# Left-over rows of a mixture of experts in units of 32 instead of 128, in plain fp32, with four column groups of TensorE

## The chip, the cores and the metric

The kernel runs on one core of a Trainium2 chip. The metric is the device time of one execution in microseconds. A core has TensorE (matmuls; PE in the profile, and PEld for its weight loads), VectorE (DVE), ScalarE (ACT), GpSimd (POOL) and SyncE (SP, which here only issues transfers). Transfers between the chip's memory and the core go through queues to 16 DMA engines. A matmul holds one operand stationary (here up to 128 rows by 128 columns), streams the other, moving one past it (here up to 512 columns), and adds into one of the eight PSUM banks that the kernel uses.

## The reference

Two layers follow each other: a retention (a linear attention with decay) and a mixture of experts with one expert per token.

```python
# retention: q, k, v are (4, 8, 768, 64)
for t in range(S):
    state = gamma * state + einsum('bhd,bhe->bhde', k[:, :, t], v[:, :, t])
    y[:, :, t] = scale * einsum('bhd,bhde->bhe', q[:, :, t], state)
x = y.transpose(0, 2, 1, 3).reshape(3072, 512)

# mixture: 8 experts, w1 (8, 512, 1024), w2 (8, 1024, 512)
logits = x @ w_gate + modality_bias[modality_id]
e_idx = argmax(logits)
gate_w = softmax(logits)[e_idx]
for e in range(E):
    mask = e_idx == e
    h = maximum(x[mask] @ w1[e], 0)
    out[mask] = gate_w[mask] * (h @ w2[e])
```

All data are fp32. Which expert a token goes to is only known on the chip.

## The kernel before, in words

**Retention and routing.** The 3072 tokens are 24 chunks of 128. For each chunk the kernel computes scores (`sc`, line 188), the state (`st`, 249), the outputs (`y`, 209 and 215), and from them the tokens' rows and router logits (`x`, 232). These matmuls are plain fp32; those of lines 188, 209, 215 and 249 use halves or quarters of the array side by side. After every three chunks the rows are routed, and scattered into `x_dram`, a region in the chip's memory where each expert has its own run of rows. Each row carries its token's number and its gate weight behind the 512 values. Rows that fill up a piece are padded with zeros and a token number that is out of bounds (`pad_c`).

**Slots and units.** A candidate is a piece of 256 rows of one expert (12 per expert, 96 in all). At five points during the retention (`EVENTS`) the two best full pieces become jobs "e"; after the last chunk the two largest pieces that are left become slots "s0" and "s1" of 256 rows, and whatever is left then is listed in units "u" of 128 rows. The lists are computed on the chip (`final_a`, `final_m`, `final_b`): one-hot matrices by rank, summed by small matmuls into a row of integers. SP reads expert and position of each job from such a list into registers (`reg`, `start_job`).

**A job.** Matmuls of the experts run in fp32r, which is made accurate by splitting each operand into a high and a low part and adding three products (`PAIRS`). So each expert's weights are loaded as eight raw pieces of 512 KB (`raw`, line 576, four of w1 and four of w2; the transfer is skipped when the job before has the same expert), and each piece is cut (`cut`): a cast on ACT (`hi`, 580) and a subtraction on DVE (`lo`, 582). A slot's first layer (`first_slot`, 636) gives eight blocks of the hidden layer, transposed as they come, 12 matmuls each; its second layer (`second`, 682) does two halves of 128 rows, 24 matmuls each; the half is scaled by the gate weight on ACT (694) and scattered to the output by POOL (695). That makes 16 steps, counted as `t` from 0: 0 to 7 the first layer, 8 to 15 the second.

A unit job (`first_unit`) has its 128 rows stationary and the weights moving: four blocks of 12 matmuls (652), each followed by a relu on ACT (659), transposes on TensorE (`flip`, 671) and splits on ACT and DVE (594, 595), then the second layer over one half.

**What sets the order.** `tc.manual_schedule` keeps PE, ACT, DVE and SP in program order; each engine works its instructions off in that order and waits where it must. The program order is that of `run_job`: while job k goes through its steps, the next job's w1 is loaded at step 2 (after the register loads), its rows and its w2 at step 8, its rows are transposed at step 12 (`flip_x`, 621), its w1 is cut at steps 9, 11, 13, 15, and job k's own w2 at steps 0, 2, 4, 6. In a unit job the same things lie closer: loads at steps 0 and 4, the transposes at step 7, the cuts at steps 0 to 7. `raw` tiles exist once, so a load waits on SP until the piece before it has been cut, and all later loads wait behind it. In between, `tick` deals out the routing and list steps, and `next(ret)` the rest of the retention.

**The jobs:** ten "e", then s0, u0, s1, u1. The first `NTAIL = 2` units are such jobs; further ones would be done by a loop at the end of the program, `For_i(NTAIL, nun)`, whose number of turns is a value read from the list. PSUM has eight banks handed out in turn.

Of the kernel before, what the change touches and what calls it, by code (L numbers as in the profile page):

```python
# [7 lines left out]
F32 = mybir.dt.float32  # L8
# [7 lines left out]
P = 128  # L16
# [14 lines left out]
NEV = 2  # L31
NFIN = NSLOT - NEV * len(EVENTS)
NTAIL = 2
NUNIT = 40
DENSE = 10
# [11 lines left out]
def kernel(  # L47
# [351 lines left out]
    ex_c = cnd[:, 2:3]  # L399
    U = NUNIT  # L400

    def small(nm, shape, dt=F32):
# [5 lines left out]
    lc = {}  # L408
    lists = {}

    def list_consts():
# [6 lines left out]
        vals = small("vals", [NCAND, 3], BF16)  # L418
# [4 lines left out]
        nc.vector.tensor_copy(vals[:, 2:3], ex_c)  # L423
        onef = small("onef", [NCAND, NCAND])
# [10 lines left out]
        nc.gpsimd.memset(base_f[:, n : n + U], float(EMPTY))  # L435
        lc.update(ord_r=ord_r, vals=vals, onef=onef, base_e=base_e, base_f=base_f)
        mid["keep"] = keep
# [27 lines left out]
    def ranked():  # L465
# [5 lines left out]
        rank = passing("rank", [NCAND, 1])  # L471
        nc.vector.tensor_reduce(rank, gt, axis=AX.X, op=ALU.add)
        return size, rank

# [25 lines left out]
    def final_a():  # L500
        size, rank = ranked()
        ord_r = lc["ord_r"]
        h0 = small("h0", [NCAND, 1])
        nc.vector.tensor_scalar(h0, size, 0.0, None, op0=ALU.is_gt)
        h0b = small("h0b", [NCAND, 1], BF16)
        nc.vector.tensor_copy(h0b, h0)
# [4 lines left out]
        rku = small("rku", [NCAND, 1])  # L511
        nc.vector.tensor_scalar(rku, rank, float(NFIN), None, op0=ALU.subtract)
        h1 = small("h1", [NCAND, 1])
        nc.vector.tensor_scalar(h1, size, float(P), None, op0=ALU.is_gt)
        lft = small("lft", [NCAND, 1])
        nc.vector.tensor_scalar(lft, rku, 0.0, None, op0=ALU.is_ge)
        nc.vector.tensor_tensor(h1, h1, lft, op=ALU.mult)
        nc.vector.tensor_tensor(h0, h0, lft, op=ALU.mult)
        mid["f"] = (ohs, h0, h0b, h1, rku)

    def final_m():
        ohs, h0, h0b, h1, rku = mid.pop("f")
# [7 lines left out]
        rk1 = small("rk1", [NCAND, 1])  # L530
        nc.vector.scalar_tensor_tensor(
            rk1, pn[:NCAND, 0:1], float(-NFIN), rku, op0=ALU.add, op1=ALU.add
        )
        oh1 = small("oh1", [NCAND, U], BF16)
        nc.vector.tensor_scalar(oh1, ord_r, rk1, h1, op0=ALU.is_equal, op1=ALU.mult)
        h0c = small("h0c", [NCAND, 1], BF16)
        nc.vector.tensor_copy(h0c, h0)
        h1c = small("h1c", [NCAND, 1], BF16)
        nc.vector.tensor_copy(h1c, h1)
        mid["f"] = (ohs, oh0, oh1, h0c, h1c)  # L540

    def final_b():
        ohs, oh0, oh1, h0c, h1c = mid.pop("f")
        vals = lc["vals"]
# [7 lines left out]
        for i in range(3):  # L552
            mm(i * NFIN, NFIN, vals[:, i : i + 1], ohs, True, True)
        mm(n, U, vals[:, 0:1], oh0, True, False)
        mm(n, U, vals[:, 1:2], oh1, False, True)
        mm(n + U, U, vals[:, 2:3], oh0, True, False)
        mm(n + U, U, vals[:, 2:3], oh1, False, True)
        mm(n + 2 * U, 1, h0c, one, True, False)
        mm(n + 2 * U, 1, h1c, one, False, True)
        w = n + 2 * U + 1  # L560
# [82 lines left out]

    def first_unit(s):
        tag, hT = s["tag"], s.setdefault("hT", [])
        hs = []
        for i in range(4):
            ph = bank(f"uh{i}_{tag}")[:, :256]
            n = 0
            for kc in range(KC):  # L650
                for a, wi in PAIRS:
                    nc.tensor.matmul(
                        ph, s["xT"][kc // 2][a][:, kc % 2, :],
                        s["w1"][i][wi][:, kc * 256 : (kc + 1) * 256],
                        start=(n == 0), stop=(n == 3 * KC - 1),
                    )
                    n += 1
            t = me.tile([P, 256], F32, tag="hs", name=f"hs{i}_{tag}", bufs=2)
            nc.scalar.activation(t, ph, AF.Relu)
            hs.append(t)  # L660
            if i > 0:
                flip(tag, i - 1, hs[i - 1], hT)
            if i < 3:
                yield
        flip(tag, 3, hs[3], hT)
        yield

    def flip(tag, i, hs, hT):
        pb = bank(f"ut{i}_{tag}")
        for m in range(2):  # L670
            nc.tensor.transpose(pb[:, m * P : (m + 1) * P], hs[:, m * P : (m + 1) * P], ident)
        for m in range(2):
            hT.append(split("hT", 2 * i + m, pb[:, m * P : (m + 1) * P], [P, P]))

    def second(s):
        tag, hT = s["tag"], s["hT"]
        for hh in range(s["nh"]):
# [26 lines left out]
            )  # L704
            if tag != "dyn":
                disjoint(ins, "out_rows")
            yield

    def reg(lst, i, hi):
        return nc.values_load(lst[0:1, i : i + 1], engines=[SP], min_val=0, max_val=hi)  # L710

    def start_job(j):
        kind, g, i = j
        s = dict(tag=f"{kind}{g}{i}", nh=1 if kind == "u" else 2)
        if kind == "e":
            lst, at, n = lists[g], 0, NEV
            s["group"] = g
        elif kind == "s":
            lst, at, n = lists["final"], 0, NFIN
        else:  # L720
            lst, at, n = lists["final"], 3 * NFIN, U
        s["e"] = reg(lst, at + s["nh"] * n + i, NE - 1)
# [12 lines left out]
    def both(s):  # L735
        yield from first_slot(s) if s["nh"] == 2 else first_unit(s)
        yield from second(s)
# [3 lines left out]
    def run_job(k):  # L741
        cur = state_of[k]
        long = cur["nh"] == 2
        last = k + 1 == len(jobs)
        if not long:
            cuts = {t: (cur, 2, t) for t in range(4)}
        elif k == 0:
            cuts = {0: (cur, 1, 2), 1: (cur, 1, 3)}
# [4 lines left out]
        for t, _ in enumerate(both(cur)):  # L753
            if t == (2 if long else 0) and not last:
                nxt = state_of[k + 1] = start_job(jobs[k + 1])
                raw(nxt, 1, cur)
                for i in range(4):
                    cuts[9 + 2 * i if long else 4 + i] = (nxt, 1, i)
            if t in cuts:
                cut(*cuts[t])  # L760
            if not last:
                if t == (8 if long else 4):
                    rows_in(nxt)
                    raw(nxt, 2, cur)
                if t == (12 if long else 7):
                    flip_x(nxt)
# [102 lines left out]
    def everything():  # L869
# [11 lines left out]
        decay_v(0)  # L881
        ret = retention(modi)

        ahead = None
# [19 lines left out]
        for k in range(len(jobs)):  # L904
            for t, _ in enumerate(run_job(k)):
                if t % 2:
                    tick()
                if t % 3 == 1:
                    next(ret, None)
        assert next(ret, None) is None and not todo  # L910

# [6 lines left out]
    with tc.For_i(NTAIL, nun, 1) as iv:  # L918
# [3 lines left out]
        cd = nc.values_load(  # L922
            lst[0:1, bass.ds(iv + at, 1)], engines=[SP], min_val=0, max_val=EMPTY
        )
        s = dict(tag="dyn", nh=1, e=e, at=[cd])
        rows_in(s)
        raw(s, 1)
        raw(s, 2)
        flip_x(s)
        for m in (1, 2):  # L930
            for i in range(4):
                cut(s, m, i)
        for _ in both(s):
            pass
# [89 lines left out]
```

## Time and profile before

| | us |
|---|---|
| three runs: median, lowest, highest | 475.86, 470.4, 477.1 |
| the profiled execution: its own time | 472.48 |
| its span, first to last instruction | 470.5 |
| TensorE busy | 433.6 (92%) |
| VectorE busy | 287.0 (61%) |
| ScalarE busy | 205.9 (44%) |
| mean rate of the DMA engines | 182 GB/s |

The profile shows one execution. Its lines give start and duration in us, engine, source line, operation, `output<-inputs`, and in square brackets how long the engine stood idle before and for whom. `PEclk` is the TensorE clock that was granted, as a share of full speed. In tables by stretch the columns are: length of the stretch, then busy time and number of instructions for PE, PEld, DVE, ACT and POOL, the granted clock, the busy share of the DMA engines and GB/s. Matmuls are pipelined, so a record's duration (0.28 us) is longer than the spacing of two records (0.12 us); it is the spacing that tells what a matmul costs in a row of them. Records of tiles of job u0 and u1 carry the names `xp_u`, `uh_u`, `ut_u`, `o_u`; those of s0 and s1 end in `_s`, those of early jobs in `_e`.

### The profile page before, as it was taken

The numbers are of one execution on the slowest core, as the hardware profiler recorded it, in microseconds if no ns is written. First come the engines' busy times: TensorE is split into PE (matmuls) and PEld (weight loads), VectorE is DVE, ScalarE is ACT, GpSimd is POOL, SyncE is SP. The second block draws the span as 40 slices with busy tenths as digits, with TensorE's granted clock in tenths as the row PEclk, the third lists the DMA queues.
The fourth block names the chain that finished last, engine by engine and source line by source line (L and its number), as shares of the span: only waits on it lengthen the run. The fifth ranks groups of instructions, "written<-read, shape, count | busy, mean of one in ns | idle before, by whom it ended". The sixth has DMA issues, their size and how long they took to land.

```text
span 470.5 us, 10222 instructions
## 1 busy us (share of the span) xinstructions
PE 433.6 (92%) x3676; PEld 382.9 (81%) x3676; DVE 287.0 (61%) x648; ACT 205.9 (44%) x363; POOL 103.1 (22%) x130
## 2 busy tenths in 40 slices
PE   3997989998999999999999999979999999889980
PEld 3876879888889889879879889878989898779860
DVE  1787488658556856855765677436656564667350
ACT  1221135445335336245345455435646464755540
POOL 2225215023011310421141042760000000000100
PEclk9998689999999999999999999999999999989987
DMA  8993797933535683348412171724757313864100
GB/s 287 400 362 118 273 396 241 388 129 116 162 113 176 230 340 114 128 150 292 139 69 97 45 230 65 257 71 158 256 196 255 106 48 119 286 240 163 71 1 2
DMA packets 27860, 85.70 MB, mean 182 GB/s; under 512 B 5278, under 2 KB 5406, under 8 KB 27808
## 3 DMA queue, kind: packets, MB, share of 16 engines
q1 hardware_dynamic: 22240, 70.50, 43.1%
q0 software_dynamic: 5280, 14.10, 7.9%
q8 instruction: 30, 0.49, 0.4%
q10 hardware_dynamic: 288, 0.43, 0.3%
q14 instruction: 22, 0.18, 0.1%
HBM read 91.61 MB, written 18.24 MB: 233 GB/s over the span
## 4 chain that ended last, share of the span: by engine, by line
PE 47%; issue 34%; DVE 6%; POOL 6%; DMA 3%; ACT 1%; POOLq 0%; ACTq 0%; DVEq 0%
PE h_e L636 13%; PE o_e L682 12%; PE sc L188 5%; PE x L232 5%; PE y L215 5%; POOL out_dram L695 3%; PE y L209 3%; POOL x_dram L386 3%; PE st L249 2%; DVE lo_e L582 2%; DMA kq<-in_qkv_dram 1%; DMA x_dram<-zer,pad_i 1%; PE xp_e L621 1%; ACT hi_e L580 1%; DVE a L193 1%
## 5 line engine op out<-in xcount | busy, mean ns | idle before, releaser
L582 DVE TENSOR_TENSOR lo_e<-raw,hi_e 128x1024 fp32r<-128x1024 f32 x80 | 98.1, 1226 | 66.7 <-ACT hi_e L580 57.1
L636 PE MATMUL h_e<-xTh,lo_e 128*128 128x256 f32 x320 | 91.4, 286 | 3.2 <-DVE lo_e L582 1.7
L636 PE MATMUL h_e<-xTh,hi_e 128*128 128x256 f32 x320 | 93.0, 290 | 0.5 <-issue 0.3
L636 PE MATMUL h_e<-xTl,hi_e 128*128 128x256 f32 x320 | 91.2, 285 | 0.7 <-issue 0.7
L580 ACT CAST hi_e<-raw 128x1024 fp32r<-128x1024 f32 x80 | 83.5, 1043 | 0.0
L682 PE MATMUL o_e<-hi_e,hTh 128*128 128x512 f32 x160 | 65.7, 411 | 0.0
L636 PEld LDWEIGHTS h_e<-xTh,lo_e 128*128 128x128 f32 x320 | 62.0, 194 | 3.4 <-DVE lo_e L582 2.3
L636 PEld LDWEIGHTS h_e<-xTh,hi_e 128*128 128x128 f32 x320 | 61.9, 193 | 2.9 <-issue 1.6
L636 PEld LDWEIGHTS h_e<-xTl,hi_e 128*128 128x128 f32 x320 | 61.9, 194 | 1.4 <-issue 1.3
L682 PE MATMUL o_e<-lo_e,hTh 128*128 128x512 f32 x160 | 62.7, 392 | 0.0
L682 PE MATMUL o_e<-hi_e,hTl 128*128 128x512 f32 x160 | 62.6, 391 | 0.0
L589 ACT ACTIVATE hTh<-h_e 128x256 fp32r<-128x256 f32 x80 | 30.6, 384 | 61.9 <-PE h_e L636 52.7
L779 POOL TENSOR_TENSOR vd<-kv,cst 128x512 f32<-128x512 f32 x24 | 25.4, 1060 | 107.8 <-PE y L215 59.1
L193 DVE TENSOR_TENSOR a<-sc,cst 128x512 f32<-128x512 f32 x48 | 30.8, 683 | 24.1 <-PE sc L188 24.0
L590 DVE SCALAR_TENSOR_TENSOR hTl<-h_e,hTh 128x256 fp32r<-128x256 f32 x80 | 33.3, 418 | 18.5 <-ACT hTh L589 18.1
L695 POOL DMA_INDIRECT out_dram<-o_e,xg_e x20 | 19.9, 995 | 111.1 <-ACT o_e L694 103.0
L694 ACT ACTIVATE o_e<-o_e,xg_e 128x512 f32<-128x512 f32 x20 | 13.8, 689 | 68.4 <-issue 36.7
L188 PE MATMUL sc<-kq 64*128 64x128 f32 x384 | 30.6, 303 | 7.5 <-DMA kq<-in_qkv_dram 7.5
L326 POOL DMA_INDIRECT x_dram<-xs,pos x24 | 29.3, 1220 | 33.1 <-DVE key L458 18.1
L682 PEld LDWEIGHTS o_e<-hi_e,hTh 128*128 128x128 f32 x160 | 30.1, 188 | 7.5 <-issue 1.4
L682 PEld LDWEIGHTS o_e<-lo_e,hTh 128*128 128x128 f32 x160 | 30.0, 188 | 6.7
L682 PEld LDWEIGHTS o_e<-hi_e,hTl 128*128 128x128 f32 x160 | 30.1, 188 | 5.2
(171 smaller groups left out, 724.4 us busy)
## 6 DMA issues: line engine op xcount, KB each, us to landing
raw<-in_w_dram SPq DMA_DIRECT2D x112, 512.0 KB
kv<-in_qkv_dram SPq DMA_DIRECT2D x24, 512.0 KB
kq<-in_qkv_dram SPq DMA_DIRECT2D x23, 512.0 KB
xg_e<-x_dram SPq DMA_DIRECT2D x20, 272.0 KB
xg_s<-x_dram SPq DMA_DIRECT2D x4, 272.0 KB
xg_u<-x_dram SPq DMA_DIRECT2D x2, 272.0 KB
x_dram<-xs,pos POOLq DMA_INDIRECT x24
out_dram<-o_e,xg_e POOLq DMA_INDIRECT x20
```

The costliest lines, as they stand in the source:

```text
L188: nc.tensor.matmul(pe[j][:, g * P : (g + 1) * P], kt[r, g], qt[r, g], start=True, stop=True, skip_group_check=True,)
L193: nc.vector.tensor_tensor(a[:, j], pe[j].rearrange("p (h t) -> p h t", t=P), mask.unsqueeze(1).to_broadcast([P, NG, P]), op=ALU.mult,)
L215: nc.tensor.matmul(py[j][g % 2 * D : (g % 2 + 1) * D, g // 2], vd[:, 2 * g + j], a[:, j, g], start=(s is None and g < 2), stop=(g >= 2), s ...
L326: ins = nc.gpsimd.indirect_dma_start(out=x_dram[:, :], out_offset=bass.IndirectOffsetOnAxis(ap=pos[:, i : i + 1], axis=0), in_=xs.rearrang ...
L580: nc.scalar.copy(hi, raws[m][i])
L582: nc.vector.tensor_tensor(lo, raws[m][i], hi.bitcast(F32), op=ALU.subtract)
L589: nc.scalar.activation(hi, src, AF.Relu)
L590: nc.vector.scalar_tensor_tensor(lo, src, 0.0, hi.bitcast(F32), op0=ALU.max, op1=ALU.subtract)
L636: nc.tensor.matmul(ph, s["w1"][f // 2][wi][:, o : o + P], s["xT"][kc // 2][a][:, kc % 2, :], start=(n == 0), stop=(n == 3 * KC - 1),)
L682: nc.tensor.matmul(po, hT[f][a][:, hh * P : (hh + 1) * P], s["w2"][f // 2][wi][:, (f % 2) * DM : (f % 2 + 1) * DM], start=(n == 0), stop=( ...
L695: ins = nc.gpsimd.indirect_dma_start(out=out[:, :], out_offset=bass.IndirectOffsetOnAxis(ap=xg.bitcast(I32)[:, 0, P : P + 1], axis=0), in_ ...
L779: ins = nc.gpsimd.tensor_tensor(vds[n], vv, dec[:, n % NCH].unsqueeze(2).to_broadcast([P, H, D]), op=ALU.mult)
```

## The change

Left-over rows are listed in units of 32 rows instead of 128, up to 144 of them, and a unit is no job any more. `jobs` holds the ten "e" and s0, s1; `first_unit`, `flip` and the unit's branches in `start_job` and `run_job` are removed. A new generator `unit` does one unit: it loads the expert's weights whole and unsplit into rooms that the retention used (`kq`, `kv`, `a`), and computes in plain fp32. The first layer's four quarters of 256 hidden columns go to four column groups of 32 (output partitions 0 to 31, 32 to 63, and so on of one bank), so that the hidden layer of 32 rows fills 128 partitions; the second layer's four partial sums come out in the same way, and a matmul with a constant 0/1 matrix `sel` adds the four groups. The main loop deals the unit's stages out: unit 0's loads at step 9 of the last early job, its stages at steps 3, 6, 8, 10, 12 of s0; unit 1's loads at step 9 of s0, its stages in s1. The loop at the end, for further units, calls the same generator without a slot beside it.

```diff
+UNIT = 32
 NTAIL = 2
-NUNIT = 40
+NUNIT = 144
...
+        nc.vector.tensor_reduce(
+            sel, ident.rearrange("p (j t) -> p t j", t=UNIT), axis=AX.X, op=ALU.add
+        )
...
     def final_m():
...
         pn = bank("pn")
-        one = ones[:NCAND, :NCAND]
-        nc.tensor.matmul(pn[:NCAND, 0:1], one, h0b, start=True, stop=True)
-        oh0 = small("oh0", [NCAND, U], BF16)
-        nc.vector.tensor_scalar(oh0, ord_r, rku, h0, op0=ALU.is_equal, op1=ALU.mult)
...
+        nc.tensor.matmul(pn[:NCAND, 0:1], mid.pop("lt"), numb, start=True, stop=True)
+        end = small("end", [NCAND, 1])
+        nc.vector.tensor_tensor(end, pn[:NCAND, 0:1], num, op=ALU.add)
+        first = small("first", [NCAND, 1])
+        nc.vector.tensor_copy(first, pn[:NCAND, 0:1])
...
+        ohu = small("ohu", [NCAND, U], BF16)
+        nc.vector.tensor_scalar(ohu, ord_r, first, None, op0=ALU.is_ge)
         nc.vector.scalar_tensor_tensor(
...
+            ohu, ord_r, end, ohu, op0=ALU.is_lt, op1=ALU.mult
+        )
+        at = small("at", [NCAND, U], BF16)
+        nc.vector.tensor_tensor(at, ohu, ord_r, op=ALU.mult)
...
+    def unit(tag, e, at):
+        wa = [ld.tile([P, QW], F32, tag="kq", name=f"wa{i}_{tag}", bufs=4) for i in range(4)]
+        wb = [ld.tile([P, QW], F32, tag="kv", name=f"wb{i}_{tag}", bufs=3) for i in range(3)]
+        wb.append(wk.tile([P, QW], F32, tag="a", name=f"wb3_{tag}"))
+        xu = wk.tile([UNIT, NG, P + NE], F32, tag="xs", name=f"xu_{tag}", bufs=6)
+        nc.sync.dma_start(
+            xu.rearrange("p g e -> p (g e)"), x_dram[bass.ds(at * UNIT, UNIT), :]
+        )
+        for src, w in ((w1, wa), (w2, wb)):
+            for i in range(4):
+                nc.sync.dma_start(w[i], src[bass.ds(e, 1), i].rearrange("o p f -> p (o f)"))
+        yield
+        pb = bank(f"ux_{tag}")[:, : KC * UNIT].rearrange("p (k t) -> p k t", k=KC)
+        for kc in range(KC):
+            nc.tensor.transpose(pb[:, kc], xu[:, kc, :P], ident[:UNIT, :UNIT])
+        xT = wk.tile([P, KC, UNIT], F32, tag="s", name=f"uxT_{tag}")
+        nc.vector.tensor_copy(xT, pb)
+        yield
+        ph = bank(f"uh_{tag}")
+        for kc in range(KC):
+            for j in range(4):
+                nc.tensor.matmul(
+                    ph[j * UNIT : (j + 1) * UNIT, :256], xT[:, kc],
+                    wa[j][:, kc * 256 : (kc + 1) * 256],
+                    start=(kc == 0), stop=(kc == KC - 1), skip_group_check=True,
+                )
+        hs = wk.tile([P, 256], F32, tag="s", name=f"uhs_{tag}")
+        nc.scalar.activation(hs, ph[:, :256], AF.Relu)
+        yield
+        pt = bank(f"ut_{tag}")
+        for m in range(2):
+            nc.tensor.transpose(pt[:, m * P : (m + 1) * P], hs[:, m * P : (m + 1) * P], ident)
+        hT = wk.tile([P, 2, P], F32, tag="s", name=f"uhT_{tag}")
+        nc.vector.tensor_copy(hT, pt[:, :256].rearrange("p (m t) -> p m t", m=2))
+        yield
+        po = bank(f"uo_{tag}")
+        for m in range(2):
+            for j in range(4):
+                nc.tensor.matmul(
+                    po[j * UNIT : (j + 1) * UNIT], hT[:, m, j * UNIT : (j + 1) * UNIT],
+                    wb[j][:, m * DM : (m + 1) * DM],
+                    start=(m == 0), stop=(m == 1), skip_group_check=True,
+                )
+        os = wk.tile([P, DM], F32, tag="yT", name=f"uos_{tag}")
+        nc.scalar.copy(os, po)
+        yield
+        pf = bank(f"uf_{tag}")[:UNIT]
+        nc.tensor.matmul(pf, sel, os, start=True, stop=True)
+        of = wk.tile([UNIT, DM], F32, tag="yT", name=f"uof_{tag}")
+        nc.scalar.activation(of, pf, AF.Copy, scale=xu[:, 0, P + 1 : P + 2])
+        ins = nc.gpsimd.indirect_dma_start(
...
     jobs = [("e", g, i) for g in EVENTS for i in range(NEV)]
-    for i in range(max(NFIN, NTAIL)):
-        jobs += [("s", 0, i)] * (i < NFIN) + [("u", 0, i)] * (i < NTAIL)
+    jobs += [("s", 0, i) for i in range(NFIN)]
+
+    steps = {}
+    for u in range(NTAIL):
+        k = len(jobs) - NTAIL + u
+        steps[k - 1, 9] = u
+        steps.update({(k, t): u for t in (3, 6, 8, 10, 12, 14)})
...
                 if t % 3 == 1:
                     next(ret, None)
+                if (k, t) in steps:
+                    u = steps[k, t]
+                    if u not in units:
+                        at = 3 * NFIN + u
+                        lst = lists["final"]
+                        units[u] = unit(
+                            f"u{u}", reg(lst, at + U, NE - 1), reg(lst, at, NCAND * UPS)
+                        )
+                    next(units[u], None)
...
     with tc.For_i(NTAIL, nun, 1) as iv:
...
-        for _ in both(s):
+        for _ in unit("dyn", e, cd):
             pass
```

The list steps `final_a`, `final_m` and `final_b` change with it: a piece of `size` rows gives as many units as there are multiples of 32 below `size`, and the units are numbered through by a matmul with the comparison matrix of the ranks.

More of the change, by code (lines that the diff above doesn't have):

```diff
@@ L533, in final_m @@
         )
[L534 to L540, printed above, removed]
+        at = small("at", [NCAND, U], BF16)
+        nc.vector.tensor_tensor(at, ohu, ord_r, op=ALU.mult)
+        mid["f"] = (ohs, numb, back, ohu, at)
@@ L542, in final_b @@
     def final_b():
-        ohs, oh0, oh1, h0c, h1c = mid.pop("f")
+        ohs, numb, back, ohu, at = mid.pop("f")
         vals = lc["vals"]
@@ L553, in final_b @@
             mm(i * NFIN, NFIN, vals[:, i : i + 1], ohs, True, True)
[L554 to L559, printed above, removed]
+        mm(n, U, vals[:, 3:4], ohu, True, False)
+        mm(n, U, one, at, False, False)
+        mm(n, U, back, ohu, False, True)
+        mm(n + U, U, vals[:, 2:3], ohu, True, True)
+        mm(n + 2 * U, 1, numb, one, True, True)
         w = n + 2 * U + 1
@@ L642, in first_slot @@
             yield
[L644 to L673, printed above, removed]
     def second(s):
@@ L713, in start_job @@
         kind, g, i = j
-        s = dict(tag=f"{kind}{g}{i}", nh=1 if kind == "u" else 2)
+        s = dict(tag=f"{kind}{g}{i}", nh=2)
         if kind == "e":
@@ L717, in start_job @@
             s["group"] = g
-        elif kind == "s":
+        else:
             lst, at, n = lists["final"], 0, NFIN
-        else:
-            lst, at, n = lists["final"], 3 * NFIN, U
         s["e"] = reg(lst, at + s["nh"] * n + i, NE - 1)
@@ L735, in both @@
     def both(s):
-        yield from first_slot(s) if s["nh"] == 2 else first_unit(s)
+        yield from first_slot(s)
         yield from second(s)
@@ L742, in run_job @@
         cur = state_of[k]
-        long = cur["nh"] == 2
         last = k + 1 == len(jobs)
-        if not long:
-            cuts = {t: (cur, 2, t) for t in range(4)}
-        elif k == 0:
+        if k == 0:
             cuts = {0: (cur, 1, 2), 1: (cur, 1, 3)}
@@ L753, in run_job @@
         for t, _ in enumerate(both(cur)):
-            if t == (2 if long else 0) and not last:
+            if t == 2 and not last:
                 nxt = state_of[k + 1] = start_job(jobs[k + 1])
@@ L757, in run_job @@
                 for i in range(4):
-                    cuts[9 + 2 * i if long else 4 + i] = (nxt, 1, i)
+                    cuts[9 + 2 * i] = (nxt, 1, i)
             if t in cuts:
@@ L882, in everything @@
         ret = retention(modi)
+        units = {}
         ahead = None
@@ L922 @@
         cd = nc.values_load(
-            lst[0:1, bass.ds(iv + at, 1)], engines=[SP], min_val=0, max_val=EMPTY
+            lst[0:1, bass.ds(iv + at, 1)], engines=[SP], min_val=0, max_val=NCAND * UPS
         )
[L925 to L932, printed above, removed]
-        for _ in both(s):
+        for _ in unit("dyn", e, cd):
             pass
```

55 lines of the change are left out of this document (36 added, 19 removed).

## The prediction, on record before the changed kernel was run

> **What bounds the kernel now.** I read the page first, then stretches of the end cut at the starts of its jobs, then TensorE's records in order, then the DMA issues.
>
> ```profile
> span 470.5 us, 10222 instructions
> PE 433.6 (92%) x3676; PEld 382.9 (81%) x3676; DVE 287.0 (61%) x648; ACT 205.9 (44%) x363; POOL 103.1 (22%) x130
> ...
> PEclk9998689999999999999999999999999999989987
> ```
>
> TensorE is busy 92% of the span and nobody else is near; its granted clock has dents only at the start and in the last slices. These hold the left-over jobs, so I cut there: job e9 (the last early slot), slot s0, unit u0, slot s1, unit u1, and what follows the last matmul.
>
> ```profile
> core 0: us, PE busy (x) PEld busy (x) DVE busy (x) ACT busy (x) POOL busy (x), PEclk, DMA share, GB/s
> 353.10:376.41 23.31, 23.31 (x153) 21.35 (x152) 13.67 (x18) 12.90 (x20) 1.96 (x2) 1.00 0.53 182
> 376.41:399.32 22.91, 22.91 (x149) 20.92 (x148) 13.13 (x18) 12.40 (x20) 1.96 (x2) 1.00 0.25 82
> 399.32:415.56 16.24, 13.97 (x82) 12.24 (x81) 11.04 (x16) 11.16 (x21) 0.98 (x1) 0.89 0.73 246
> 415.56:443.55 27.99, 25.80 (x157) 23.37 (x156) 15.06 (x21) 13.53 (x22) 1.96 (x2) 0.94 0.49 172
> 443.55:459.70 16.15, 13.91 (x81) 12.08 (x79) 8.08 (x13) 8.34 (x18) 0.98 (x1) 0.89 0.04 13
> 459.70:470.50 10.80, 0.16 (x1) 0.00 (x0) 0.00 (x0) 0.69 (x1) 0.98 (x1) 0.70 0.01 2
> ```
>
> A slot is 23.31 us of unbroken matmuls at full clock (e9). A unit holds TensorE for 16.2 us, and the slot after one takes 27.99. Where the extra goes is in TensorE's waits, and in what follows each of them:
>
> ```profile
> 408.17 0.44 PE L671 MATMUL ut_u<-cst,hs_u 128*128 128x128 f32 x2 [2.27 <-ACT hs_u L659]
> 417.92 0.38 PE L636 MATMUL h_s<-xTh,hi_s 128*128 128x256 f32 x1 [1.32 <-ACT xTh L594]
> 419.29 0.39 PE L636 MATMUL h_s<-xTl,hi_s 128*128 128x256 f32 x1 [0.87 <-DVE xTl L595]
> 452.34 0.44 PE L671 MATMUL ut_u<-cst,hs_u 128*128 128x128 f32 x2 [2.24 <-ACT hs_u L659]
> ```
>
> ```profile
> 409.46:412.87 3.41, 3.41 (x10) 2.67 (x9) 2.27 (x5) 3.02 (x6) 0.00 (x0) 0.51 0.51 169
> 419.70:423.11 3.41, 3.41 (x18) 3.41 (x18) 0.70 (x3) 1.32 (x2) 0.00 (x0) 0.51 0.87 319
> 453.83:457.24 3.41, 3.41 (x10) 2.67 (x9) 1.97 (x4) 1.31 (x3) 0.00 (x0) 0.51 0.00 0
> ```
>
> Each gap of about 2.2 us is followed by 3.41 us at a clock of 0.51, in which half, 1.7 us, is lost. So three gaps and three such stretches, some 6.7 + 5.1 us, stand in the end beside the units' own matmuls. TensorE's order bounds this end; what takes time out of its row between 376.41 and 459.70 comes off the span.
>
> **What falls away.** From 376.41 to the last matmul's end stand 22.91 + 16.24 + 27.99 + 16.15 = 83.29 us. Both 128-row units go, with 16 casts and 16 subtractions of their weights. Slot s1 now follows s0 directly, its rows transposed at s0's step 12 with steps 13 to 15 as cover, as in e9; the x wait at 417.92 goes with it. Two slots remain: s0 as e9, 23.31; s1 without a next job's 8 transposes:
>
> ```profile
> 348.09 1.04 PE L621 MATMUL xp_e<-cst,xg_e 128*128 128x128 f32 x8
> 348.89 0.48 PE L682 MATMUL o_e<-hi_e,hTh 128*128 128x512 f32 x1
> ```
>
> These take 348.89 - 348.09 = 0.80, so s1 is 22.51.
>
> **What comes: a unit of 32 on TensorE.** The trace has plain fp32 matmuls in the retention, full width and side by side:
>
> ```profile
> 115.29 0.93 PE x L232 x8
> 116.22 0.60 PE y L209 x16
> 116.81 1.02 PE y L215 x16
> 117.84 4.50 PE h_e L636 x36
> ```
>
> An fp32 matmul leaves two records (4 matmuls of line 232 are 8 records). Those of 128x128 by 136 columns go one after another: 0.93 / 8 / 136 = 0.855 ns per column and record. Line 215 has two groups of 64 columns over all 128 rows: 16 records of 128 columns would be 1.75 us alone and took 1.02, which is 8 rounds of pairs (0.875) and 0.15 on entering. Line 209 has four 64x64 quarters: 4 rounds (0.44) and 0.16. The 36 matmuls behind them took 4.50 where 36 spacings of 0.12 make 4.32, so coming back costs 0.18:
>
> ```profile
> 375.96 0.39 PE L682 MATMUL o_e<-hi_e,hTl 128*128 128x512 f32 x1
> 376.19 0.39 PE L682 MATMUL o_e<-lo_e,hTh 128*128 128x512 f32 x1
> ...
> 376.52 0.28 PE L636 MATMUL h_s<-xTh,lo_s 128*128 128x256 f32 x1
> 376.64 0.28 PE L636 MATMUL h_s<-xTl,hi_s 128*128 128x256 f32 x1
> ...
> 394.76 0.60 PE L621 MATMUL xp_u<-cst,xg_u 128*128 128x128 f32 x4
> 395.12 0.48 PE L682 MATMUL o_s<-hi_s,hTh 128*128 128x512 f32 x1
> ...
> 446.43 0.38 PE L671 MATMUL ut_u<-cst,hs_u 128*128 128x128 f32 x2
> 446.56 0.36 PE L652 MATMUL uh_u<-hi_u,xTh 128*128 128x256 f32 x1
> ```
>
> The unit, stage by stage, each with 0.16 to enter and 0.18 to return:
> - rows transposed: four, of 32 rows, at most the 0.36 of four full ones: 0.70
> - first layer: 16 matmuls are 32 records of 256 columns; four abreast, 8 rounds x 256 x 0.855 ns = 1.75: 2.09
> - hidden transposed: two, 0.13, and 0.1 after: 0.25
> - second layer: 8 matmuls are 16 records of 512 columns; four abreast, 4 rounds = 1.75: 2.09
> - the sum over the groups: 2 records of 512 columns = 0.88: 1.22
>
> Together U = 6.35 us. No row shows four groups of 32 over the same 128 rows. Bounds: everything abreast and free to enter, 4.9; pairs only, as line 215 shows, 3.5 us for each layer, U = 9.85; one after another 7.0 each, U = 16.85. I take four abreast: line 209 shows four in flight, and line 215 that groups sharing all rows do not hinder each other.
>
> On this the Trainium skill ("TensorE: Matmul & The Clock Gate", Part 3, Measured speedup vs the span model) has three column groups of 512 columns at 2.38x, not 3x. At that efficiency four would be 3.17x, each layer 2.2 us, and the sum would come out 1.8 us higher; an estimate from that page, and line 215's pairs (1.75 in 0.875 beside the entry) do better than it.
>
> **Copies on ACT and DVE.**
>
> ```profile
> L694 ACT ACTIVATE o_e<-o_e,xg_e 128x512 f32<-128x512 f32 x20 | 13.8, 689 | 68.4 <-issue 36.7
> ...
> L659 ACT ACTIVATE hs_u<-uh_u 128x256 f32<-128x256 f32 x8 | 3.1, 386 | 0.0
> L595 DVE TENSOR_TENSOR hTl<-ut_u,hTh 128x128 fp32r<-128x128 f32 x16 | 4.4, 287 | 2.7 <-ACT hTh L594 2.7
> ```
>
> A unit adds 0.39 + 2 x 0.69 on ACT and two copies on DVE of 0.29 to 0.42. ACT is busy 12.40 and DVE 13.13 of s0's 22.91, and between a unit's stages stand two steps of the slot (one of 12 spacings, 1.44, and six of 0.23, 1.4). The relu needs the cut and split ahead of it plus itself, some 1.9 us, and has 2.8. I cost these at nothing, covered by the slot's matmuls. Without that cover each of four copies per unit would hold TensorE about 1 us, 8 in all, and gaps that long would bring the half clock back.
>
> **The weights on SP's queue.**
>
> ```profile
> q1 hardware_dynamic: 22240, 70.50, 43.1%
> ...
> raw<-in_w_dram SPq DMA_DIRECT2D x112, 512.0 KB
> ...
> xg_u<-x_dram SPq DMA_DIRECT2D x2, 272.0 KB
> ```
>
> ```profile
> 10.00:20.00 10.00, 10.00 (x151) 8.98 (x148) 6.35 (x19) 1.89 (x5) 3.51 (x10) 1.00 1.04 397
> 20.00:30.00 10.00, 9.15 (x150) 7.96 (x151) 9.33 (x36) 2.40 (x7) 2.96 (x7) 1.00 1.03 408
> ```
>
> A unit adds its rows (70 KB) and eight loads of 512 KB, unconditional, behind slot s0's (or s1's) second-layer weights and ahead of the next slot's first-layer ones. The order is kept, so those next ones queue behind 4.2 MB: 10.5 us at 400 GB/s. u0's loads can start once s0's last w2 piece has its room, after e9's step 6 (about 364), and their rooms are free since the retention; they land near 376, wanted from s0's step 6 (near 387). Slot s1's w1 follows by about 382, wanted from step 9 (near 391); its w2 by 390, wanted from 406. u1's first rooms come free at u0's first layer (388), its second at u0's second layer (395); all land by 406 and are wanted from 416. Nothing sits behind u1's waits on SP. The early jobs see none of this. I cost the loads at nothing; if DMA gave 182 GB/s, the page's mean, the 13.2 MB from 365 on would land at 438 where the last are wanted near 425: 13 us.
>
> **Lists.** The final lists grow to 144 places and need some more DVE operations of this kind, once, near 280; TensorE's wait there now:
>
> ```profile
> 280.78 0.23 PE L550 MATMUL ptf<-oh,vals 96*1 96x40 bf16 x3 [0.22 <-DVE h0c L537]
> ```
>
> I add 0.4 for that and the new constant's reduction at the start, between 0 and 1.
>
> **The sum.** 472.48 (the profiled execution) - 83.29 + 23.31 + 22.51 + 2 x 6.35 + 0.4 = 448.1; I say 448. What follows the last matmul (10.80) and the 1.98 us outside the span stay, since the last output is again a 128-row one. The profiled execution is 3.4 below the median of the runs (475.86) and 2.1 above the fastest, so no correction.
>
> **How many units there are** decides whether the loop at the end runs. It does not now (no row of it; 112 loads are 14 jobs). Two units of 128 can be up to eight of 32. From the reference's own inputs I worked out the router's counts: 1567, 1502 and 3 rows. Six slots go to each large expert, the last of 222 rows; 31 and 3 rows are left: two units either way. The trace bears this out: 70.50 MB less 24 + 23.5 retention loads of 0.524 MB, 26 row loads of 0.279 and 0.6 of the rest leaves 37.7 MB = 72 pieces, nine loads of an expert, as many as this order of jobs has.
>
> **Rivals.**
> - *The groups do not run side by side.* Pairs: 448.1 + 2 x 3.5 = 455.1. One at a time: 448.1 + 2 x 10.5 = 469.1, no change that can be told. For it: no row with four over the same rows. Against: lines 215 and 209. The Trainium skill speaks for it ("TensorE: Matmul & The Clock Gate", Part 3, The mechanism): a weight load overlaps running matmuls only where the row group differs, and all groups here share their rows. The trace differs for pairs, 1.02 us against 1.75.
> - *Weights late*, as costed: 13 us, 461. Against: 397 and 408 GB/s in the profile.
> - *Slower: the loop runs.* Each further unit there is bare: 4.2 MB (10.5 us), U, copies of 2.4, and no cover, 21 us or more. One turn gives 469, two 490; from two on it is slower than before. For it: a unit is a quarter as large and there are still two in the schedule. Against: the counts.
>
> **How the numbers follow.** Forecast 0.72, pairs 0.10, one at a time 0.06, late weights 0.05, the loop twice or more 0.04, and 0.03 for something better than the forecast (free entry and no list cost, 445, or less). A measurement of this kernel tells about 2% from no change. Faster by more: 0.72 + 0.10 + 0.05 + 0.03 less a little = 0.89; within: 0.06; slower: 0.05. The range goes from 442 (445 less the runs' 0.7%) to 457 (pairs plus the list and the runs' scatter).
>
> **What would show it.** Right: two last slots near 29.7 and 28.9 us, granted clock 1.00 through them, no wait of 2 us on TensorE after 376, the first layer's 32 records in about 2 us, 96 raw loads and 16 of the unit's. Wrong: these records in 3.5 or 7 us; a TensorE wait on a unit's weights or copies; a third unit's rows.

## The result, and the profile after

The changed kernel takes 448.31 us (median of 4 runs, 446.39 to 450.31); the ratio to the kernel before is 0.9517, interval 0.9449 to 0.9585. Run once more on another chip, beside the kernel before on the same one, it took 443.53 against 465.8: 0.9511, interval 0.9475 to 0.9546. Chips differ by some 2% for the kernel before (464.8 to 476), so only ratios of one chip are compared below. The ratios are those on record, formed from fast executions alone (one of 833.93 us of the kernel before is left out) and not from the medians shown (448.31 / 475.86 would be 0.942), and the profiled execution of the kernel before counts as a slow one.

The page of the changed kernel, first the busy time of TensorE, then the granted clock in 40 slices, then the weight loads:

```profile
span 444.4 us, 9973 instructions
PE 414.1 (93%) x3619; PEld 358.7 (81%) x3619; DVE 265.5 (60%) x619; ACT 185.7 (42%) x323; POOL 103.9 (23%) x130
...
PEclk9999598999999999999999999999999999999996
...
raw<-in_w_dram SPq DMA_DIRECT2D x96, 512.0 KB
...
wa_u<-in_w_dram SPq DMA_DIRECT2D x8, 512.0 KB
wb_u<-in_w_dram SPq DMA_DIRECT2D x8, 512.0 KB
```

The dents of the clock in the last slices are gone, except behind the last matmul. The end in stretches: slot s0 with unit 0 in it, slot s1 with unit 1, and what follows the last matmul (columns as before):

```profile
375.22:404.74 29.52, 29.52 (x210) 23.41 (x208) 14.47 (x20) 14.53 (x23) 2.85 (x3) 1.00 1.02 398
404.74:433.33 28.59, 28.59 (x201) 22.28 (x199) 9.69 (x15) 10.65 (x18) 2.85 (x3) 1.00 0.06 23
433.33:444.40 11.07, 0.16 (x1) 0.00 (x0) 0.00 (x0) 0.69 (x1) 0.98 (x1) 0.65 0.05 19
```

TensorE is busy without a gap at full clock for 58.11 us, where the same end took 83.29 in the kernel before. That is 25.18 us. The profiled executions differ by 472.48 - 446.39 = 26.09; the rest is s0 starting 1.19 earlier and the tail being 0.27 longer. These are one profile of each kernel. On the second chip the medians differ by 465.8 - 443.53 = 22.3 us; why that is 2.9 less than the end's 25.18 is not shown. All that TensorE waited for from 300 us on, in total, times and longest:

```profile
PE xp_e L637 <- DMA xg_e<-x_dram: 0.6, 2, 0.4
PE o_e L667 <- DVE lo_e L598: 0.5, 1, 0.5
```

Both lie ahead of s0. A unit's first layer within its slot, from TensorE's records, and the groups of both units' matmuls in the two layers:

```profile
385.73 0.28 PE L652 MATMUL h_s<-xTl,hi_s 128*128 128x256 f32 x1
385.94 1.94 PE L717 MATMUL uh_u<-wa_u,uxT_u 128*32 128x256 f32 x32
387.80 0.39 PE L652 MATMUL h_s<-xTh,hi_s 128*128 128x256 f32 x1
```

```profile
L717 PE MATMUL uh_u<-wa_u,uxT_u 128*32 128x256 f32 x64 | 3.9, 382 | 0.0
L734 PE MATMUL uo_u<-wb_u,uhT_u 128*32 128x512 f32 x32 | 3.8, 598 | 0.0
```

The 32 records of a first layer would take 7.0 us one by one at 0.855 ns per column; they take 1.95.

### The profile page after: what moved, and what is told of

Read it like the earlier page. It is cut to its first block, busy times and chain, and to the rows that moved or that the text cites. A ratio compares the mean times of both kernels' runs of the same rounds, so it can differ in the third digit from the quotient of the medians.

```text
span 444.4 us, 9973 instructions
## 1 busy us (share of the span) xinstructions
PE 414.1 (93%) x3619; PEld 358.7 (81%) x3619; DVE 265.5 (60%) x619; ACT 185.7 (42%) x323; POOL 103.9 (23%) x130
## 4 chain that ended last, share of the span: by engine, by line
PE 56%; issue 20%; DVE 8%; DMA 6%; POOL 5%; ACT 2%; SPq 0%; POOLq 0%; ACTq 0%; DVEq 0%
PE h_e L652 17%; PE o_e L667 16%; PE sc L190 6%; PE x L234 5%; PE y L217 5%; PE y L211 3%; POOL x_dram L388 2%; DVE lo_e L598 2%; PE st L251 2%; DMA x_dram<-zer,pad_i 2%; POOL out_dram L680 2%; ACT hi_e L596 2%; DMA kq<-in_qkv_dram 1%; DMA raw<-in_w_dram 1%; PE xp_e L637 1%
```

## The experiments

TensorE's matmuls ahead of slot s0 are the same in the runs made from the changed kernel, yet s0 starts anywhere from 370.9 to 379.0 us in their profiles. That scatter hides a few microseconds. So each run is judged first by its end: from s0's first matmul to the end of the last one (the last record's start plus 0.23 us; where the last are the two records of `uf`, the first one's start plus 0.86).

| run | s0 starts | end, us | median us | ratio to before, same chip |
|---|---|---|---|---|
| kernel before | 376.41 | 83.29 | 475.86 | |
| changed kernel | 375.22 | 58.11 | 448.31 | 0.9517 |
| after_again | 374.43 | 58.11 | 443.53 | 0.9511 |
| no_units | 370.94 | 45.74 | 430.15 | 0.9292 |
| one_group | 372.77 | 63.48 | 448.92 | 0.9662 |
| pairs | 374.01 | 59.91 | 445.75 | 0.959 |
| same_column | 372.08 | 70.88 | 455.97 (1 run) | |
| double_loads | 371.43 | 101.92 | 485.78 | 1.046 |
| extra_traffic | 372.12 | 60.44 | 445.39 | 0.9574 |
| not_dealt | 373.81 | 64.4 | 452.84 | 0.9639 |
| before_no_gap | 372.60 | 80.57 | 465.76 | 0.9877 |
| one_turn | 378.97 | 59.8 | 448.17 | 0.9506 |
| two_turns | 371.50 | 82.1 | 461.04 | 0.9874 |
| no_sum | 371.06 | 55.70 | 440.16 | 0.9452 |

**after_again.** No edit.

> The changed kernel once more, as the measure for the other runs of this call: from the start of slot s0 to the last matmul 58.1 us (it was 58.11), whatever the stages before take.

The end is again 58.11 us, to the hundredth, on another chip and with another start of s0. So differences of a few tenths in this column mean something.

**no_units: what do the units cost?**

```diff
-                if (k, t) in steps:
+                if False and (k, t) in steps:
```

> Leaves out both units (loads, matmuls, copies and their output rows: 34 of 3072 rows are not computed). My theory: a unit costs only the time of its matmuls on TensorE (6.05 us each by the profile of the changed kernel), everything else is covered: 446.4 - 12.1 = 434.3 us. Rival (loads and copies also cost something, in the slots or before them): clearly less, 431 or lower. Rival (part of the units' matmuls already lies in gaps): 437 or more.

The slots by themselves:

```profile
370.94:394.26 23.32, 23.32 (x154) 21.36 (x152) 13.66 (x18) 12.91 (x20) 1.97 (x2) 1.00 0.55 183
394.26:416.68 22.42, 22.42 (x145) 20.34 (x143) 8.98 (x13) 9.02 (x15) 1.97 (x2) 1.00 0.06 24
```

45.74 us, so both units cost 58.11 - 45.74 = 12.37, or 6.19 each; their five stages add up to 6.05 in the records. A unit costs its matmuls and what entering and leaving them takes, no more. The whole time, 430.15, is lower than expected and lies in the rival's range, but that chip was faster for the kernel before too (464.79); the end alone tells the two apart. By the same measure the units of the kernel before cost 83.29 - 45.74 = 37.55.

**one_group and pairs: does the order of the groups matter?**

```diff
-        for kc in range(KC):
-            for j in range(4):
+        for j in range(4):
+            for kc in range(KC):
                 nc.tensor.matmul(
                     ph[j * UNIT : (j + 1) * UNIT, :256], xT[:, kc],
...
-        for m in range(2):
-            for j in range(4):
+        for j in range(4):
+            for m in range(2):
```

> Only the order of the unit's matmuls is changed: in both layers all matmuls of one column group come before those of the next, so that neighbours share a group. My theory (groups run abreast when neighbours in the order are in different groups): a unit's first layer takes 7.0 us instead of 1.95, its second 7.0 instead of 1.94, since 32 records of 256 columns (16 of 512) at 0.855 ns each per column follow one another; 2 x 10.1 us more, 466.5 against 446.4 us in the profiled execution. Rival (TensorE picks whichever group is free, whatever the order, by its pulling weight loads ahead): no change, 446 to 448.

In `pairs` the order is `[(c, i + b) for b in (0, 2) for c in range(KC) for i in range(2)]`, and likewise in the second layer.

> The order of the unit's matmuls lets only two column groups alternate: groups 0 and 1 through the whole layer, then 2 and 3. My theory: each layer takes 3.5 us plus 0.2, 2 x 3.4 us more, 453 against 446.4 us. Rival (four abreast never was, two do as well as four): no change. Rival (order does not matter): no change.

The groups of matmuls, the first two lines from one_group, the third from pairs:

```profile
L717 PE MATMUL uh_u<-wa_u,uxT_u 128*32 128x256 f32 x64 | 9.2, 382 | 0.0
L734 PE MATMUL uo_u<-wb_u,uhT_u 128*32 128x512 f32 x32 | 3.9, 598 | 0.0
```

```profile
L717 PE MATMUL uh_u<-wa_u,uxT_u 128*32 128x256 f32 x64 | 5.6, 382 | 0.0
```

By these records my theory fell, and so did the rivals. With eight records of one group in a row a first layer takes 4.6 us, neither 1.95 nor 7.0; with four in a row (the second layer) it takes as long as in alternation. Counting the records in flight in stretches of 0.9 us (length, busy time and count, clock, DMA) shows how; first one_group, then the changed kernel:

```profile
383.40:384.30 0.90, 0.82 (x4) 1.00 1.00 391
384.30:385.20 0.90, 0.90 (x10) 1.00 1.08 426
...
387.00:387.90 0.90, 0.90 (x6) 1.00 1.02 410
```

```profile
385.85:386.75 0.90, 0.81 (x16) 1.00 0.99 390
386.75:387.65 0.90, 0.90 (x24) 1.00 1.08 427
```

At first one group runs alone, four records in 0.9 us; then two groups run abreast, ten or eleven in each 0.9 us, and at the end one. Each group starts when the one before it starts its fifth record (384.38 and 384.37 us for the first two). A reading that fits all four numbers: records are handed out in program order, each group holds about four, and when the next record's group is full, everything behind waits. Then one_group's first layer is three delays of four records (4 x 256 x 0.855 ns = 0.88) and eight records of the last group (1.75), 4.4 us beside the entry; pairs is 0.88 + 1.75 = 2.6, measured 2.8; four in a row delay nothing. That reading is worked out from these runs, and no run was made to test it alone.

**same_column: what are the four groups worth?**

```diff
-                    ph[j * UNIT : (j + 1) * UNIT, :256], xT[:, kc],
+                    ph[(j if kc == 0 else 0) * UNIT :][:UNIT, :256], xT[:, kc],
...
-                    po[j * UNIT : (j + 1) * UNIT], hT[:, m, j * UNIT : (j + 1) * UNIT],
+                    po[(j if m == 0 else 0) * UNIT :][:UNIT], hT[:, m, j * UNIT : (j + 1) * UNIT],
```

> After each column group's first matmul, all of a unit's matmuls go to group 0 (the hidden values and the sums of the 34 rows are then wrong). Theory now (each group is its own row of work, of which TensorE takes up whatever is free; the earlier order test fell because its groups still ran side by side): the first layer has 0.43 us abreast and 24 records of 0.2155 us in one group, 5.8 us with the entry; the second 0.86 abreast and 8 records of 0.43, 4.5 us; 6.4 us more per unit, 70.9 from s0's start to the last matmul. Rival (side by side was never what made it cheap): 58.

```profile
L717 PE MATMUL uh_u<-wa_u,uxT_u 128*32 128x256 f32 x64 | 11.6, 382 | 0.0
L734 PE MATMUL uo_u<-wb_u,uhT_u 128*32 128x512 f32 x32 | 9.0, 598 | 0.0
```

5.8 and 4.5 us per unit, and an end of 70.88 us where 70.9 was expected. The same number of matmuls, of the same shapes, costs 12.8 us more when they have to share a column group. So side by side is what makes the units cheap, in every order tried in which no group gets more than four records in a row.

**double_loads and extra_traffic: are the loads hidden?** In double_loads each piece is loaded twice into its tile.

```diff
-                nc.sync.dma_start(w[i], src[bass.ds(e, 1), i]...)
+                for _ in range(2):
+                    nc.sync.dma_start(w[i], src[bass.ds(e, 1), i]...)
```

> Each of the unit's 16 weight pieces is loaded twice into the same place, 8.4 MB more. My theory (loads hidden, with some 9 to 15 us of slack): 446 to 449 us, the next slot's first-layer weights coming at most 2 us late. Rival (the queue of SP is on the path): 10.5 us more per unit, 457 to 467.

The end is 44 us longer than in the changed kernel. SP's own waits in this run, and its issues; behind them the issues of the changed kernel:

```profile
SPq L707 <- DMA wa_u<-in_w_dram: 36.5, 8, 7.0
SPq L707 <- DMA wb_u<-in_w_dram: 28.6, 8, 3.9
```

```profile
363.28 21.80 SPq L707 DMA_DIRECT2D wa_u<-in_w_dram  x8
385.27 18.94 SPq L707 DMA_DIRECT2D wb_u<-in_w_dram  x8
406.65 2.56 SPq L592 DMA_DIRECT2D raw<-in_w_dram  x4
```

```profile
367.05 1.94 SPq L706 DMA_DIRECT2D wa_u<-in_w_dram  x4
369.18 2.73 SPq L706 DMA_DIRECT2D wb_u<-in_w_dram  x4
374.19 4.53 SPq L592 DMA_DIRECT2D raw<-in_w_dram  x4
```

The second load of a piece writes where the first is still landing, so SP waits for each, and unit 0 holds SP until 404. Slot s1's first-layer weights behind it are issued at 406.65 instead of 374.19. The experiment did not test the transfers' rate; it shows what waits at this place in SP's queue cost, 65.1 us of them in all. extra_traffic doubles the bytes without a second load into the same tile: behind each load the piece is also copied to a spare place in the chip's memory.

```diff
+                nc.sync.dma_start(scr[i if src is w1 else 4 + i], src[bass.ds(e, 1), i]...)
```

> Behind each of the unit's weight loads the same 512 KB are copied once more, to a spare place in the chip's memory, through the same queue and waiting for nothing: 8.4 MB more, without the waits that the doubled loads brought on SP. My theory of the prediction (loads have 9 us and more of slack, it is waits on SP that cost): at most 3 us more from s0's start to the last matmul, 58 to 61. Rival (the transfers' rate is on the path): 10.5 us per unit less the slack, 65 or more.

Two stretches of 20 us from 380 on, and TensorE's waits in the end; behind them SP's issue of slot s1's first-layer weights:

```profile
380.00:400.00 20.00, 19.08 (x133) 13.22 (x132) 8.22 (x11) 9.27 (x15) 1.19 (x2) 1.00 1.00 403
400.00:420.00 20.00, 20.00 (x160) 17.73 (x159) 10.91 (x16) 9.15 (x16) 1.66 (x2) 1.00 1.03 425
```

```profile
PE xp_s L637 <- DMA xg_s<-x_dram: 0.9, 2, 0.6
```

```profile
382.28 3.71 SPq L592 DMA_DIRECT2D raw<-in_w_dram  x4
```

8.4 MB more, at 403 and 425 GB/s in these stretches, lengthen the end by 2.33 us, to 60.44. Other than expected, the run is not free of waits on SP: it waits some 14 us at the two lines of the unit's loads and copies. Slot s1's first-layer weights are issued 10.2 us behind s0's start, where the changed kernel issues them 1.0 us ahead of it. TensorE waits for none of these weights all the same. Against the records of the changed kernel, 1.3 of the 2.33 us are lost at slot s1's rows, which stand behind them in the queue, and 1.0 within unit 1's second layer. So those weights have at least the slack of 9 us that the prediction gave them, and the rows and unit 1's own weights are what comes late first. The loads do use their room: in the changed kernel the DMA engines are busy through all of s0 (share 1.02, 398 GB/s).

**not_dealt: does it matter that the stages lie within the slot?**

```diff
-        steps.update({(k, t): u for t in (3, 6, 8, 10, 12, 14)})
+        steps.update({(k, t): u for t in (15,)})
...
                     next(units[u], None)
+                    if t == 15:
+                        for _ in units[u]:
+                            pass
```

> The changed kernel with each unit's stages all issued one after another behind its slot instead of within it; loads where they were. My theory (the slot's matmuls cover four copies per unit, which then stand bare at 0.55 to 0.9 us each): 2.8 us more per unit, 452 against 446.4 us, and up to 455 if the gaps bring half clock. Rival (dealing out is not what makes it cheap): 446 to 448. Rival (my price of a missing cover, 1 us each with half clock after): 454 to 458.

TensorE's waits from s0 on:

```profile
PE uh_u L717 <- DVE uxT_u L712: 3.2, 2, 2.9
PE uf_u L743 <- ACT uos_u L740: 1.6, 2, 0.8
PE ut_u L727 <- ACT uhs_u L723: 1.2, 2, 0.6
PE uo_u L734 <- DVE uhT_u L729: 1.0, 2, 0.5
```

7.0 us of waits, an end 6.3 us longer, and no half clock (1.00 in both slots). Unit 1's bare copies cost 0.38 to 0.84 us each, 2.3 together. Unit 0's were dearer by the one wait of 2.86, where DVE had another subtraction (1.23 us, itself behind a cast on ACT) ahead of the copy.

**before_no_gap: do the gaps bring the half clock?** Made from the kernel before.

```diff
-        flip(tag, 3, hs[3], hT)
+        s["late"] = lambda: flip(tag, 3, hs[3], hT)
         yield
...
+                if f == 3 and "late" in s:
+                    s.pop("late")()
                 if f % 2 and f < FC - 1:
                     yield
```

> The kernel before with one edit: in a unit job the last block's two transposes are issued after the first 12 matmuls of the second layer instead of ahead of them, so that TensorE has work while ACT finishes the block's relu. My theory (a gap of 2.2 us costs itself and 3.41 us at half clock after it): the two waits of 2.27 and 2.24 us go or shrink below 1 us, the half-clock stretches in u0 and u1 go too, the one in s1 stays: 472.5 - 4.5 - 3.4 = 464.6, up to 466. Rival (half clock has another cause, such as the unit's own matmuls): 468.

Unit u0, slot s1, unit u1:

```profile
395.52:410.65 15.13, 12.99 (x81) 10.95 (x80) 9.27 (x15) 10.28 (x21) 0.99 (x1) 1.00 0.77 261
410.65:439.22 28.57, 25.80 (x157) 23.37 (x156) 16.93 (x22) 14.32 (x23) 2.43 (x2) 0.94 0.52 171
439.22:453.17 13.95, 12.95 (x81) 10.78 (x79) 8.10 (x13) 8.34 (x18) 0.98 (x1) 1.00 0.04 15
```

The clock is 1.00 in both units, where it was 0.89, and still 0.94 in s1, whose gap I left. So the half clock went with the gap and is no property of the units' matmuls. The saving was smaller than expected: u0 1.1 us, u1 2.2, s1 0.6 worse, 2.7 in all. In u0 waits of 0.23, 0.92 and 0.98 came in place of the 2.27, in u1 0.20 and 0.80 in place of the 2.24, so the last splits were late next. With 1.7 us of half clock each that would still save 1.8 and 2.9; some 0.7 us per unit I can't place. The ratio is 0.9877, interval 0.98 to 0.9955.

**one_turn and two_turns: what does the loop at the end cost?** `NTAIL` is 1, then 0.

> The changed kernel with one unit within the last slot and the other left to the loop at the end, so that it makes one turn. My price of a turn was 21 us or more: 446.4 - 6.05 + 21 = 461. If TensorE has gone to half clock during the load, its 6 us become 12: 467. Rival (a turn overlaps its load with the last slot, the loop being free to start): 450.

> Both units left to the loop at the end, which makes two turns. The price of my rival in the prediction, 21 us or more for each turn behind the last slot: 446.4 - 12.4 + 42 = 476, slower than the kernel before. Theory now (the first turn's loads run ahead during the last slot, as the run with one turn showed, and only the later turn waits for rooms and transfers): 8.2 us for the first turn, 8.2 and some 7 to 12 of waiting for the second, 446.4 - 12.4 + 16.4 + 7 to 12 = 457 to 462.

With one turn SP had its loads out long before the last slot ended, and the turn ran straight behind the slot:

```profile
414.94 2.07 SPq L706 DMA_DIRECT2D wa_dyn<-in_w_dram  x4
422.77 2.02 SPq L706 DMA_DIRECT2D wb_dyn<-in_w_dram  x4
```

```profile
430.97 0.43 PE L710 MATMUL ux_dyn<-cst,xu_dyn 32*128 32x32 f32 x4
```

The end is 1.6 us longer than with both units dealt out, as the rival said. With two turns, the last slot, the first turn and the second; then TensorE's wait and SP's first issue for the second turn:

```profile
394.81:417.10 22.29, 22.29 (x145) 20.34 (x143) 8.98 (x13) 9.01 (x15) 1.96 (x2) 1.00 0.34 138
417.10:425.40 8.30, 6.00 (x58) 2.01 (x56) 0.72 (x2) 1.81 (x4) 0.98 (x1) 1.00 0.07 24
425.40:453.70 28.30, 10.76 (x56) 3.47 (x56) 0.72 (x2) 1.50 (x3) 0.88 (x1) 0.64 0.42 153
```

```profile
PE ux_dyn L710 <- DMA xu_dyn<-x_dram: 11.9, 1, 11.9
435.20 0.34 SPq L701 DMA_DIRECT2D xu_dyn<-x_dram  x1
```

The first costs 8.3 us, the second 28.3: at the loop's head SP waits 12.4 us for the output rows of the first turn, so it issues the second's loads only 10 us after the first turn's last matmul, and over this turn the clock is 0.64. The whole is 461.04 us, ratio 0.9874 (0.9821 to 0.9927): not slower than before. That it lies in the expected 457 to 462 is luck. The second turn was expected at 15 to 20 us, and the end is 82.1; but s0 began 3.7 us earlier than in the changed kernel's profile, and what follows the last matmul took 5.0 us where it took 11.07.

**no_sum: a version without the sum over the groups.** Each column group takes a quarter of the output columns and runs through all eight pieces of the hidden layer.

```diff
-        for m in range(2):
-            for j in range(4):
+        for m in range(2):
+            for i in range(4):
+                for j in range(4):
+                    o = m * DM + j * P
                     nc.tensor.matmul(
+                        po[j * UNIT : (j + 1) * UNIT], hT[:, m, i * UNIT : (i + 1) * UNIT],
+                        wb[i][:, o : o + P],
...
-        nc.tensor.matmul(pf, sel, os, start=True, stop=True)
...
+            out=out.rearrange("n (g c) -> (n g) c", g=4),
+            out_offset=bass.IndirectOffsetOnAxis(ap=idx[:, 0:1], axis=0),
```

> A version that may be better: the second layer's four column groups take a quarter of the output columns each, all eight pieces of the hidden layer one after another (64 records of 128 columns, again 1.75 us abreast), so that no sum over the groups is needed; the output is scattered in quarter rows, with token numbers and gate weights loaded once per group. The matmul with the constant matrix and the copy ahead of it go: 1.17 us per unit on TensorE, 55.8 from s0's start to the last matmul against 58.1. Rival (the four small loads per unit or the quarter rows cost as much): 57 to 59.

```profile
L749 PE MATMUL uo_u<-wb_u,uhT_u 128*32 128x128 f32 x128 | 3.9, 274 | 0.0
```

The second layer takes what it took, and the sum's 1.17 us per unit is gone: an end of 55.70 where 55.8 was expected. The median is 440.16 us, ratio 0.9452 (0.9409 to 0.9495), beside 443.53 and 0.9511 (0.9475 to 0.9546) for the changed kernel on the same chip. The intervals overlap a little; the end, 2.41 us shorter, is clear.

## Why the prediction was right, step by step

- **What bounds the end.** TensorE's row did, and what came out of it came off the span: 25.18 us there, 26.09 in the whole. same_column shows it from the other side: 12.8 us more of TensorE's work made the end 12.8 longer.
- **The sum.** The foretold end is 23.31 + 22.51 + 12.7 = 58.52, measured 58.11. That the median of 448.31 met 448 so closely is luck: s0's start alone scatters by 8 us.
- **The unit's matmuls.** U was 6.35; measured 6.05 as a sum of stages (0.55, 2.05, 0.23, 2.05, 1.17) and 6.19 by leaving the units out. Four abreast was the open choice; same_column shows it carries 12.8 us. The rule of the Trainium skill that spoke against it ("TensorE: Matmul & The Clock Gate", Part 3, The mechanism) also has matmuls start strictly in program order; here later ones of another group start ahead of earlier ones: in one_group the second group's first record starts at 384.38 us, ahead of the sixth of the first group's eight (384.59).
- **The slots.** 23.31 and 22.51 were taken; no_units has 23.32 and 22.42. With the units in them 29.7 and 28.9 were foretold, 29.52 and 28.59 measured.
- **Gaps and half clock.** Gone, as forecast. Of the 37.55 us of the old units, 6.7 were gaps and some 5.1 half clock; the other 25.7 are matmuls, 12.9 per unit against 6.2. So about half of the gain is lost time that went away, and half is smaller work. The split is worked out from one trace of the kernel before; before_no_gap bears out that clock and gaps hang together, not each microsecond. No run dealt the old units of 128 rows out within the slots, so what the dealing out alone would have brought there is not shown.
- **Copies at nothing.** Right with the cover. Without it not_dealt paid 7.0 us, where 8 and half clock were the price; the half clock did not come, though one of the gaps, 2.86 us, was longer than those of the kernel before.
- **Loads at nothing.** Right, and doubling their traffic, with the later issues that it brings, costs 2.33 us. The prediction said that nothing sits behind u1's waits on SP; double_loads shows that unit 0's place in the queue was the one that mattered.
- **Lists, 0.4.** Not shown. TensorE waited 0.9 us on the new chain's first matmul, 0.7 more than at the lists of the kernel before; s0's start scatters by 8 us.
- **The price of the slower rival was wrong:** "each further unit there is bare", 469 with one turn, 490 with two. The first turn's loads run during the last slot, so it costs 8.3 us and not 21, which gives 456; the second costs 28.3, more than said, as SP waits for the first turn's output rows. Two further turns are thus 36.6 us and not 42, 485 by the same sum. So by these numbers the rival stays slower than before from the second turn on. The whole times say the same: two_turns has no unit in its slots, and with the 12.4 us of two units dealt out its 461.04 would be 473.4, beside 465.58 for the kernel before on that chip. That is an estimate; no run had four units. None of it touched the sum, as the two units were dealt out.

## What to carry to other kernels

A small remainder is best put as filler into the row of the engine that is full, its stages far enough apart that every copy ends in time; here that made 34 rows cost their matmuls and nothing else. With few rows against wide weights, let the rows stand still and the weights stream past them, in column groups side by side; an order of matmuls that alternates the groups was safe here. No run tried the rows on the moving side. Before loads are added to a queue, look at what stands behind them: issues that came 11 us late cost 2.3 us here, those that came 36 us late 44.

## What the runs showed of the hardware that was not expected

- Four records in a row of one column group delay the others by nothing (3.9 us for both units' second layers against 3.8), eight in a row turn a layer of 1.95 us into 4.6. Room for about four records per group, filled from the program's order, would fit that.
- A loop's first turn can have its transfers issued during the straight code ahead of it (16 us before its first matmul in one_turn), while the next turn's were issued 10 us after the first had ended, behind a wait of 12.4 us on SP for the first turn's output rows.
- A stretch of 3.41 us at half clock followed gaps of about 2.2 us in the kernel before. A wait of 2.86 us in not_dealt was followed by none. What makes the difference stays open.
